# Batch 0's output in four accumulators, begun before batch 1's second attention, and output work shared out anew over the slots

## Chip, core and metric

One core of one Trainium2 chip runs the whole program. The metric is the time of one execution on the device in microseconds (us), lower is better. The kernel before takes 245.6 us, the median of three runs (245.07, 245.60 and 245.72).

## What is computed

Eight batches of 8 heads, 576 positions, head size 64. Each batch goes through two attentions: 32 learned queries `p` read keys and values and give 32 packed vectors per head, and then the real queries read these packed vectors as keys and as values. The rows of all batches (4608 x 512) go through a layer of 512 to 2048 to 512 with the function `h cos(h)` between.

```python
p_packed = sm_attn(p, k, v)              # sm_attn: softmax(scale * q @ k.T) @ v
out      = sm_attn(q, p_packed, p_packed)
x = out.transpose(0, 2, 1, 3).reshape(B * S, H * D)
h = x @ w_in
return (h * cos(h)) @ w_out
```

## The kernel before, in words

All matmuls are in bf16 with fp32 sums. The order of instructions is written out by hand: each engine runs its own in the order of the source, and only waits on data and buffers move them against each other.

**Per batch.** `s1` makes the scores of the first attention (TensorE, L143) and their exponentials (ScalarE, L152); `a1_pe` or `a1_xbar` transposes them, `pp` (L186) multiplies with v, `pp_T` (L198) transposes the packed vectors. `ppw` (L213) multiplies these with a quarter of `w_in` at once and writes `PPW`, so that the second attention's product and the first layer become one matmul. `s2` makes the scores of the second attention (L143), whose exponentials `a2u` (L231) are summed over keys by a matmul with ones (`sums2`, L239), then logarithm (L241), exponential (L247) and the product on VectorE (L249) give the normalised `a2n`.

**A slot.** `slot(s)` makes the hidden layer of batch s in 16 steps, one for each 128 of the 2048 hidden features. A step is four matmuls of 288 columns (`h_mm`, L263), the cosine on ScalarE (L267) and the product on VectorE (L270), which writes `gT`. Batch 0 is special: `h_one` makes 512 of its 576 positions (L289, L294, L295), in single banks, and `h_rest` the other 64 later (L303, L307, L309).

**The output and the filler.** `out_gen(b)` makes the output of a batch in chunks of 128 rows, each of 16 matmuls of 128x512 (L351), a copy to SBUF and a store. It is a generator: `fill(n)` takes its next n matmuls, wherever the source calls it. `slot` spreads its share evenly over its 16 steps (`quota`), more of it at steps that are `heavy`, and leaves `keep` matmuls over; `hooks` are other work put behind a step. An odd batch has a fifth chunk with the last 64 rows of two batches, which comes from `joint`. Batch 0's chunks 0 and 1 run interleaved by quarters of `w_out`, chunks 2 and 3 after them.

**Banks.** PSUM has eight banks here. Two (`O`) hold output chunks, and are borrowed through `bank`; the other six are either three pairs in turn (`psa`) or six single ones (`one`). `banks` switches between the two. A hidden product takes a pair.

**Loads.** They are issued by GpSimd (POOL) in the source's order (`load`, `load_w_in`, `load_w_out`). `xbar` transposes a batch's q or k by DMA from SyncE (SP), which also issues the stores, and `behind` lets POOL wait until such a transpose has landed. Batches 0 and 1 have their q, and batches 0 to 2 their k, transposed on TensorE instead (`pe_T`, L116); `pack_p` transposes the learned queries (L131).

**Around the change.** After batch 0's hidden layer come warm-up matmuls on zeros (`warm`, L391), the transposes of batch 1's q, a table load on ScalarE and `s2(1)`. The filler of batch 0 is set just ahead of `s2(1)`. Slot 1 has as hooks the second half of batch 1's `ppw`, `h_rest(0)`, `pack_p`, two transposes by DMA and the rest of batch 2's k. The lines that decide when the output begins:

```python
    warm(4, one())
    pe_T("q", 1, (ACT, V, V), (0,), own=one)
    ACT.preload_act_table_set(EXP_SET)
    pe_T("q", 1, (ACT, V, V), (1, 2), own=one)
    rest15()
    warm(3, one())
    ...
    banks(3)
    set_filler(0)
    s2(1)
    ppw(1, 0, V)
    fill(4)
```

Of the kernel before, what the change touches and what calls it, by code (L numbers as in the profile page):

```python
# [15 lines left out]
def kernel(  # L16
# [34 lines left out]
    ctx.enter_context(tc.manual_schedule())  # L51
    psum = {"stack": ctx.enter_context(ExitStack())}

    def banks(pairs):

        psum["stack"].close()
        if pairs:
            psum["A"] = psum["stack"].enter_context(tc.tile_pool(name="psA", bufs=pairs, space=PSUM))
        if pairs < 3:
            psum["H"] = psum["stack"].enter_context(tc.tile_pool(name="psH", bufs=6 - 2 * pairs, space=PSUM))  # L60

    banks(3)
# [20 lines left out]
    def copy(eng, out, in_):  # L83
        if eng is ACT:
            ACT.copy(out=out, in_=in_)  # L85
        else:
            eng.tensor_copy(out=out, in_=in_)  # L87

    def psa(dt=FP32):
        return psum["A"].tile([128, 2, 512 if dt == FP32 else 1024], dt, name="psA", tag="A")  # L90

    def load(n, b):
        bf[n, b] = bf_pool.tile([TP, H, C * D], BF16, name=n + "bf", tag=n + "bf", bufs=1 if n == "q" else 2)
        G.dma_start(out=bf[n, b], in_=srcs[n][b].rearrange("h (p c) d -> p h (c d)", c=C))
# [7 lines left out]
        nc.sync.dma_start_transpose(out=t, in_=bf[n, b].rearrange("p h x -> p (h x)"))  # L102

    def one(dt=FP32):
        return psum["H"].tile([128, 512 if dt == FP32 else 1024], dt, name="psH", tag="H")

    def pe_T(n, b, engs=(V, V, V), groups=(0, 1, 2), own=None):
        if 0 in groups:
# [14 lines left out]
    def bank(dt=FP32):  # L123
        return O.tile([128, 512 if dt == FP32 else 1024], dt, name="ot", tag="ot")
# [73 lines left out]
            nc.tensor.transpose(ps[:, i * 128:(i + 1) * 128], t[:, i * D:i * D + 128], ident)  # L198
        copy(eng, ppT[b % 2].rearrange("p i x n -> p (i x n)"), ps[:, 0:256])

    def ppw(b, n, eng=None, own=False, later=False, cuts=((0, 512),)):
        if b not in PPW:
            PPW[b] = ppw_pool.tile([128, 2, DF], BF16, name="PPW", tag="PPW")
        two = isinstance(eng, tuple)
        if own:
            ps = [bank(), bank()]
        else:
            t = psa()
            ps = [t[:, 0, :], t[:, 1, :]]
# [117 lines left out]

    def n_chunks(b):
        return 5 if b % 2 and b < B - 1 else 4

    def tail_chunk(b, c):
        osb = o_pool.tile([128, DM], FP32, name="osb")
        for i, (a, z) in enumerate(((0, 256), (256, 384), (384, 512))):
# [6 lines left out]
            for (a, z, rows), q in zip(pieces_of(b, c), (nc.sync, nc.scalar)):  # L340
                q.dma_start(out=rows[:, cols], in_=osb[a:z, cols])

    def out_gen(b):
        groups = [(0, 1), (2,), (3,)] if b == 0 else [(c,) for c in range(n_chunks(b))]
        for grp in groups:
            pss = {c: O.tile([128, DM], FP32, name="ot", tag="ot") for c in grp}
            for f0 in range(0, NFC, 4):
                for c in grp:
                    for fc in range(f0, f0 + 4):
                        w = joint[b // 2][:, fc, :] if c == 4 else gT[b][:, fc, c * 128:(c + 1) * 128]  # L350
                        nc.tensor.matmul(pss[c], w, w_out_bf[:, fc, :],  # L351
                                         start=(fc == 0), stop=(fc == NFC - 1))
                        if fc == NFC - 1:
                            osb = o_pool.tile([128, DM], FP32, name="osb")
                            copy(osb_eng[0], osb, pss[c])
                            for a, z, rows in pieces_of(b, c):
                                nc.sync.dma_start(out=rows, in_=osb[a:z, :])
                        yield

    filler = []  # L360

    def set_filler(b):
        filler.append([out_gen(b), 16 * n_chunks(b)])

    def to_do():
        return sum(n for _, n in filler)
# [58 lines left out]
    warm(1)  # L425
    pp_T(0)
    pe_T("q", 0, (V, ACT, V))
    load("q", 1)
    for n in range(4):
        load_w_out(n)  # L430
    G.dma_start(out=p_raw[:, 4:, :], in_=p_rows[:, 4:, :])
    load("k", 2)
# [7 lines left out]
    normalise(0)  # L440
    s1(1)
    ACT.preload_act_table_set(SIN_SET)
    cut_ppw, rest_ppw = ppw(0, 0, V, own=True, later=True, cuts=((0, 128), (128, 512)))
    warm(3, psa()[:, 0, :])
    cut_ppw()
    rest_ppw()
    banks(0)
    a1_pe(1, own=one)
    recips(1)
    for fc in range(13):  # L450
        h_one(0, fc)()()
        if fc in (0, 4, 8):
            ppw(0, 1 + fc // 4, (ACT, ACT if fc == 8 else V), own=True)
    c13 = h_one(0, 13)
    pp(1, ACT, own=bank)
    c13()()
    c14 = h_one(0, 14)
    c15 = h_one(0, 15, own=bank)
    pp_T(1, ACT, own=bank)
    c14()()  # L460
    rest15 = c15()
    warm(4, one())
    pe_T("q", 1, (ACT, V, V), (0,), own=one)
    ACT.preload_act_table_set(EXP_SET)
    pe_T("q", 1, (ACT, V, V), (1, 2), own=one)
    rest15()
    warm(3, one())
    load("k", 3)
    load("q", 2)
    load("v", 2)  # L470
    dup_p(4, 2 * B, G)
    banks(3)
    set_filler(0)
    s2(1)
    ppw(1, 0, V)
    fill(4)
    sums2(1, 0)
    fill(1)
    sums2(1, 1)
    rest_ppw, = ppw(1, 1, (V, V), later=True)  # L480
    fill(3)
    normalise(1)
    ACT.preload_act_table_set(SIN_SET)
    rest_ppw()
    fill(7)

    def slot(s, hooks, keep=0, heavy={}, last=None):


        left = to_do() - keep  # L490
        weight = [1 + heavy.get(fc, (0, 0))[0] for fc in range(NFC)]
        for fc in range(NFC):
            rest = h_mm(s, fc)
            if fc == NFC - 1 and last:
                last()
            rest()
            quota = (left * sum(weight[:fc + 1])) // sum(weight) - (left + keep - to_do())
            behind = min(quota, heavy[fc][1]) if fc in heavy else quota
            fill(quota - behind)
            while hooks and hooks[0][0] == fc:  # L500
                hooks.pop(0)[1]()
            fill(behind)
# [24 lines left out]
    def cross(n, b):  # L527
        return lambda: xbar(n, b)

    osb_eng[0] = ACT  # L530
    slot(1, [(2, lambda: pw2(1, 2, (ACT, V))), (4, lambda: h_rest(0)), (6, lambda: pack_p(2, 4)), (7, cross("k", 3)),
             (8, tk2), (9, cross("q", 2)), (10, lambda: pe_T("k", 2, (V, V, ACT), (2,)))], 4, {2: (1, 2), 4: (3, 5)})
    ACT.preload_act_table_set(EXP_SET)
    osb_eng[0] = V
    behind(xT["q", 2][0:1, 0, 0:1])
# [1 line left out]
    load("q", 3)  # L537
    load("k", 4)

    set_filler(1)  # L540
    fill(4)
    s1(2)
    fill(7)
# [28 lines left out]
        load(n, b)  # L572
    fill(9)
    osb_eng[0] = ACT
    slot(2, [(7, lambda: tiled(2))], 10, {7: (5, 4)}, lambda: pp_T(3, V))

    for s in range(3, B):
        nxt = s + 1 < B
        ACT.preload_act_table_set(EXP_SET)
        osb_eng[0] = V  # L580
        set_filler(s - 1)
# [64 lines left out]
```

## Time and profile before

| What | Value |
|---|---|
| Median of three runs | 245.6 us |
| The profiled execution | 245.1 us |
| Its span, first to last instruction | 243.3 us |
| Granted TensorE clock | 0.997 |
| TensorE busy | 233.8 us, 96% of the span |
| ScalarE, VectorE, GpSimd busy | 166.1, 162.0, 37.4 us |
| Output matmuls of 128x512 (L351) | 560, about 380 ns each as shown |
| Hidden products (L263) | 448 matmuls of 128x288 |
| Transfers | 37.37 MB in 64377 packets |

The span is what the trace covers; the execution is 1.8 us longer. A row of the timeline gives the start, the time from the first start to the last end, the engine, the source line, the operation, the tile written and the tiles read, the shape and how many there are; in brackets stands the idle time ahead of it and what ended it. Matmuls are pipelined: each is shown with its whole way through the array, so that 380 ns for one and 216 ns from one start to the next are no contradiction. The chain of waits is followed back from the last instruction, at each step to what released it.

### The profile page before, as it was taken

The numbers are of one execution on the slowest core, as the hardware profiler recorded it, in microseconds if no ns is written. First come the engines' busy times: TensorE is split into PE (matmuls) and PEld (weight loads), VectorE is DVE, ScalarE is ACT, GpSimd is POOL, SyncE is SP. The second block draws the span as 40 slices with busy tenths as digits, with TensorE's granted clock in tenths as the row PEclk, the third lists the DMA queues.
The fourth block names the chain that finished last, engine by engine and source line by source line (L and its number), as shares of the span: only waits on it lengthen the run. The fifth ranks groups of instructions, "written<-read, shape, count | busy, mean of one in ns | idle before, by whom it ended". The sixth has DMA issues, their size and how long they took to land.

```text
span 243.3 us, 5484 instructions
## 1 busy us (share of the span) xinstructions
PE 233.8 (96%) x2251; PEld 128.9 (53%) x2251; DVE 162.0 (67%) x256; ACT 166.1 (68%) x267; POOL 37.4 (15%) x60
## 2 busy tenths in 40 slices
PE   7789899999999999999999999999999999999994
PEld 3454354566446564556455654655455645665453
DVE  3259997787568795778758675868667878784001
ACT  2349999778478696868787687858796666773110
POOL 8432230210400041004100510030101010011000
PEclk9999999999999999999999999999999999999998
DMA  6999999999799999997999899999292111311133
GB/s 94 203 205 206 204 206 229 199 237 187 163 184 183 219 179 180 197 197 163 158 199 219 162 221 204 188 164 176 66 192 52 31 46 43 86 36 53 46 84 86
DMA packets 64377, 37.37 MB, mean 154 GB/s; under 512 B 36865, under 2 KB 59777, under 8 KB 64353
## 3 DMA queue, kind: packets, MB, share of 16 engines
q0 software_dynamic: 23152, 18.75, 51.0%
q1 hardware_dynamic: 40960, 18.16, 35.9%
q8 instruction: 17, 0.28, 0.4%
q10 hardware_dynamic: 240, 0.13, 0.2%
q14 instruction: 8, 0.06, 0.1%
HBM read 37.22 MB, written 9.44 MB: 192 GB/s over the span
## 4 chain that ended last, share of the span: by engine, by line
PE 82%; DVE 6%; ACT 1%; issue 1%; ACTq 0%
PE ot L351 50%; PE psA L263 22%; DVE gT L295 3%; PE psA L213 3%; PE psA L143 2%; PE psA L239 2%; PE ot L337 1%; PE psA L186 1%; DVE gT L270 1%; DVE PPW L87 1%; ACT cosT L267 1%; ACT cosT L294 0%; PE psA L116 0%; DVE qT L87 0%; PE psA L303 0%
## 5 line engine op out<-in xcount | busy, mean ns | idle before, releaser
L351 PE MATMUL ot<-w_out_bf,gT 128*128 128x512 bf16 x512 | 134.0, 379 | 0.0
L270 DVE TENSOR_TENSOR gT<-psA,cosT 128x576 bf16<-128x576 f32 x112 | 83.3, 757 | 21.0 <-ACT cosT L267 19.9
L267 ACT ACTIVATE cosT<-psA 128x576 bf16<-128x576 f32 x112 | 72.9, 652 | 24.9 <-PE psA L263 23.5
L263 PE MATMUL psA<-a2n,PPW 128*128 128x288 bf16 x448 | 73.3, 286 | 0.0
L351 PEld LDWEIGHTS <-gT 128*128 128x128 bf16 x512 | 48.2, 98 | 39.5 <-issue 4.2
L263 PEld LDWEIGHTS <-PPW 128*128 128x128 bf16 x448 | 43.8, 98 | 30.1 <-issue 0.4
L87 DVE CAST PPW<-psA 128x1024 bf16<-128x1024 f32 (+1 forms) x24 | 26.8, 1131 | 6.4 <-PE psA L213 6.2
L85 ACT COPY osb<-ot 128x512 f32<-128x512 f32 (+1 forms) x23 | 13.1, 569 | 16.2 <-PE ot L351 13.9
L87 DVE COPY osb<-ot 128x512 f32<-128x512 f32 (+2 forms) x15 | 9.7, 645 | 20.4 <-PE ot L337 17.2
L274 POOL COPY joint<-gT 128x512 bf16<-128x512 bf16 x14 | 8.6, 618 | 78.2 <-DVE gT L270 78.2
L249 DVE SCALAR_TENSOR_TENSOR a2n<-a2u,r,lns 128x576 bf16<-128x576 bf16 x16 | 12.4, 814 | 9.6 <-ACT lns L247 9.6
L152 ACT ACTIVATE a<-psA 128x576 bf16<-128x576 f32 x16 | 10.2, 646 | 8.2 <-PE psA L143 8.2
L241 ACT ACTIVATE lns<-psA 128x576 f32<-128x576 f32 x16 | 10.3, 650 | 7.2 <-PE psA L239 6.7
L351 PE MATMUL ot<-w_out_bf,joint 128*128 128x512 bf16 x48 | 12.2, 380 | 0.0
L98 POOL COPY gate<-kT 1x1 bf16<-1x1 bf16 x4 | 0.7, 180 | 72.7 <-DMA kT<-kbf 72.7
L231 ACT ACTIVATE a2u<-psA,rs 128x576 bf16<-128x576 f32 x16 | 11.0, 737 | 1.1 <-PE psA L143 1.0
L247 ACT ACTIVATE lns<-lns 128x576 f32<-128x576 f32 x16 | 10.0, 673 | 0.0
L213 PE MATMUL psA<-w_in_bf,ppT 64*32 64x512 bf16 x224 | 9.8, 379 | 0.0
L295 DVE TENSOR_TENSOR gT<-psH,cosT 128x512 bf16<-128x512 f32 x15 | 9.3, 680 | 0.4 <-ACT cosT L294 0.4
L391 PE MATMUL ot<-wz 128*128 128x512 f32 (+2 forms) x13 | 7.5, 661 | 1.9 <-DVE wz L404 1.7
L294 ACT ACTIVATE cosT<-psH 128x512 bf16<-128x512 f32 x15 | 8.4, 628 | 0.7 <-DVE gT L295 0.4
L289 PE MATMUL psH<-a2n,PPW 128*128 128x512 bf16 x30 | 7.8, 381 | 0.8 <-DVE PPW L87 0.8
(88 smaller groups left out, 170.6 us busy)
## 6 DMA issues: line engine op xcount, KB each, us to landing
kbf<-in_k_dram POOLq DMA_DIRECT2D x8, 576.0 KB, 14.0
vbf<-in_v_dram POOLq DMA_DIRECT2D x8, 576.0 KB, 7.8
qbf<-in_q_dram POOLq DMA_DIRECT2D x8, 576.0 KB, 10.9
out_dram<-osb SPq DMA_DIRECT2D x24, 192.0 KB, 2.6
out_dram<-osb SPq DMA_DIRECT2D x22, 128.0 KB, 2.9
w_in_bf<-in_moe_w_in_dram POOLq DMA_DIRECT2D x4, 512.0 KB, 17.3
w_out_bf<-in_moe_w_out_dram POOLq DMA_DIRECT2D x4, 512.0 KB, 20.8
out_dram<-osb SPq DMA_DIRECT2D x25, 64.0 KB, 2.3
```

The costliest lines, as they stand in the source:

```text
L85: ACT.copy(out=out, in_=in_)
L87: eng.tensor_copy(out=out, in_=in_)
L152: ACT.activation(out=a1[b % 2][:, y, :, 0:TP].rearrange("p (e m) x -> p e m x", e=2), in_=ps[y][:, :, 0:HS].rearrange("p e (m x) -> p e m ...
L213: nc.tensor.matmul(ps[y][32 * x:32 * x + 32, :], ppT[b % 2][r, 0, x, :], w_in_bf[r, x, n * 512:(n + 1) * 512], start=True, stop=True)
L231: ACT.activation(out=a2u[b][:, y].rearrange("p (e x) -> p e x", e=2), in_=ps[y][:, :, 0:HS], func=AF.Exp, scale=rs1[b][:, y:y + 1])
L241: ACT.activation(out=lns[b][:, y].rearrange("p (e x) -> p e x", e=2), in_=ps[:, :, 0:HS], func=AF.Ln)
L249: V.scalar_tensor_tensor(out=a2n[b][:, y], in0=a2u[b][:, y], scalar=r1[b][:, y:y + 1], in1=lns[b][:, y], op0=ALU.mult, op1=ALU.mult)
L263: nc.tensor.matmul(ps[:, e, 0:HS], PPW[b][:, y, fc * 128:(fc + 1) * 128], a2n[b][:, y, e * HS:(e + 1) * HS], start=(y == 0), stop=(y == 1))
L267: ACT.activation(out=csv, in_=ps[:, :, 0:HS], func=AF.Sin, bias=PI_HALF)
L270: V.tensor_tensor(out=gT[b][:, fc, :].rearrange("p (e x) -> p e x", e=2), in0=ps[:, :, 0:HS], in1=csv, op=ALU.mult)
L295: return lambda: V.tensor_tensor(out=gT[b][:, fc, 0:512], in0=ps, in1=cs, op=ALU.mult)
L351: nc.tensor.matmul(pss[c], w, w_out_bf[:, fc, :], start=(fc == 0), stop=(fc == NFC - 1))
```

## The change

Three things are changed.

- The first quarter of `w_out` is loaded ahead of batch 1's q instead of behind it.
- Batch 0's output is made by `out_first`, with all four chunks open at once. Chunks 0 and 1 take the two output banks, chunks 2 and 3 one of the three pairs, which is held (`at=2`) while the other work has two pairs in turn. The 64 matmuls go by quarters of `w_out`. They begin straight after batch 0's hidden layer; the seven warm-up matmuls there are gone, the first two `ppw` of batch 1 move ahead of its transposes and into single banks, and `c15` takes a single bank. 36 output matmuls stand ahead of slot 1 instead of 15. When chunk 3 is complete, ScalarE copies chunks 2 and 3 out and the third pair returns.
- Odd slots, and the last one, end with the first 7 or 8 matmuls of their own output: `slot` sets its own filler at step 10 (`trail`). Slot 1 gets a list of weights for its steps and its hooks stand later; what even slots leave over (`keep`) falls to 0 or 1.

The loads of later batches, the shapes and the arithmetic are the same. The diff, cut to its core:

```diff
+    pairs, turn = [], [0]
-    def banks(pairs):
+    def banks(kind):
         psum["stack"].close()
...
+        name, n = ("psA", 1) if kind == "pairs" else ("psH", 6)
+        psum[name] = psum["stack"].enter_context(tc.tile_pool(name=name, bufs=n, space=PSUM))
+        pairs[:], turn[0] = [0, 1, 2], 0
...
+    def psa(dt=FP32, at=None):
+        if at is None:
+            at = pairs[turn[0] % len(pairs)]
+            turn[0] += 1
+        return psum["psA"].tile([128, 2, 512 if dt == FP32 else 1024], dt, name="psA", tag=f"A{at}")
...
+    def out_first():
+        pss = {}
+        for c, fcs in ((0, 4), (1, 4), (2, 4), (3, 4), (0, 8), (1, 8), (2, 8), (3, 8),
+                       (2, 12), (3, 12), (2, 16), (3, 16), (0, 16), (1, 16)):
+            if c not in pss:
+                if c == 2:
+                    held = psa(at=2)
+                    pairs[:] = [0, 1]
+                pss[c] = O.tile([128, DM], FP32, name="ot", tag="ot") if c < 2 else held[:, c - 2, :]
+            for fc in range(8 if (c, fcs) in ((0, 16), (1, 16)) else fcs - 4, fcs):
+                nc.tensor.matmul(pss[c], gT[0][:, fc, c * 128:(c + 1) * 128], w_out_bf[:, fc, :],
+                                 start=(fc == 0), stop=(fc == NFC - 1))
+                if fc == NFC - 1 and c == 3:
+                    store(0, 2, pss[2])
+                    store(0, 3, pss[3])
+                    pairs[:], turn[0] = [0, 1, 2], 0
+                elif fc == NFC - 1 and c < 2:
+                    store(0, c, pss[c])
+                yield
...
+    load_w_out(0)
     load("q", 1)
-    for n in range(4):
+    for n in range(1, 4):
         load_w_out(n)
...
-    rest15 = c15()
-    warm(4, one())
-    pe_T("q", 1, (ACT, V, V), (0,), own=one)
+    c15()()
+    set_filler(0)
+    fill(4)
+    for n in range(2):
+        ppw(1, n, (ACT, V), own=one)
+    fill(4)
     ACT.preload_act_table_set(EXP_SET)
-    pe_T("q", 1, (ACT, V, V), (1, 2), own=one)
-    rest15()
-    warm(3, one())
+    banks("pairs")
+    fill(4)
+    t = psa(BF16)
+    for i in range(2):
+        pe_T("q", 1, (None,) * 3, (i,), own=lambda dt: t[:, i, :])
+    V.tensor_copy(out=xT["q", 1][:, 0:16].rearrange("p (i a) x -> p i (a x)", i=2), in_=t[:, :, 0:8 * TP])
+    pe_T("q", 1, (V, V, ACT), (2,))
...
+    fill(4)
     s2(1)
-    ppw(1, 0, V)
     fill(4)
     sums2(1, 0)
-    fill(1)
+    fill(2)
     sums2(1, 1)
-    rest_ppw, = ppw(1, 1, (V, V), later=True)
-    fill(3)
+    fill(10)
     normalise(1)
     ACT.preload_act_table_set(SIN_SET)
-    rest_ppw()
-    fill(7)
+    fill(4)
...
+            if fc == 10 and trail:
+                set_filler(s)
...
-    slot(1, [(2, lambda: pw2(1, 2, (ACT, V))), (4, lambda: h_rest(0)), (6, lambda: pack_p(2, 4)), (7, cross("k", 3)),
-             (8, tk2), (9, cross("q", 2)), (10, lambda: pe_T("k", 2, (V, V, ACT), (2,)))], 4, {2: (1, 2), 4: (3, 5)})
+    slot(1, [(5, lambda: pw2(1, 2, (ACT, V))), (6, lambda: h_rest(0)), (7, cross("k", 3)),
+             (8, lambda: pack_p(2, 4)), (9, cross("q", 2)), (10, tk2), (11, lambda: pe_T("k", 2, (V, V, ACT), (2,)))],
+         trail=8, heavy={5: (0, 2), 6: (0, 2)}, weight=[3, 3, 3, 3, 2, 3, 3, 2, 2, 2, 2, 2, 2, 2, 1, 1])
...
-    slot(2, [(7, lambda: tiled(2))], 10, {7: (5, 4)}, lambda: pp_T(3, V))
+    slot(2, [(7, lambda: tiled(2))], 0, {7: (5, 4)}, lambda: pp_T(3, V))
...
-            slot(s, [(7, lambda: tiled(s))], 5 if s % 2 else 13, {7: (5, 4)}, lambda: pp_T(s + 1, V))
+            slot(s, [(7, lambda: tiled(s))], 0 if s % 2 else 1, {7: (5, 4)}, lambda: pp_T(s + 1, V),
+                 7 if s % 2 else 0)
         else:
-            slot(s, [], 5)
-    set_filler(B - 1)
+            slot(s, [], trail=7)
     fill(1000)
```

More of the change, by code (lines that the diff above doesn't have):

```diff
@@ L52 @@
     psum = {"stack": ctx.enter_context(ExitStack())}
-    def banks(pairs):
+    pairs, turn = [], [0]
+    def banks(kind):
         psum["stack"].close()
[L57 to L62, printed above, removed]
+        name, n = ("psA", 1) if kind == "pairs" else ("psH", 6)
+        psum[name] = psum["stack"].enter_context(tc.tile_pool(name=name, bufs=n, space=PSUM))
+        pairs[:], turn[0] = [0, 1, 2], 0
+    banks("pairs")
     V, ACT, G = nc.vector, nc.scalar, nc.gpsimd
@@ L87, in copy @@
             eng.tensor_copy(out=out, in_=in_)
-    def psa(dt=FP32):
-        return psum["A"].tile([128, 2, 512 if dt == FP32 else 1024], dt, name="psA", tag="A")
+    def psa(dt=FP32, at=None):
[3 more added lines that the diff above has]
+        return psum["psA"].tile([128, 2, 512 if dt == FP32 else 1024], dt, name="psA", tag=f"A{at}")
     def load(n, b):
@@ L104, in one @@
     def one(dt=FP32):
-        return psum["H"].tile([128, 512 if dt == FP32 else 1024], dt, name="psH", tag="H")
+        return psum["psH"].tile([128, 512 if dt == FP32 else 1024], dt, name="psH", tag="H")
     def pe_T(n, b, engs=(V, V, V), groups=(0, 1, 2), own=None):
@@ L199, in pp_T, with ppw @@
         copy(eng, ppT[b % 2].rearrange("p i x n -> p (i x n)"), ps[:, 0:256])
-    def ppw(b, n, eng=None, own=False, later=False, cuts=((0, 512),)):
+    def ppw(b, n, eng=None, own=None, later=False, cuts=((0, 512),)):
         if b not in PPW:
@@ L205, in ppw @@
         if own:
-            ps = [bank(), bank()]
+            ps = [own(), own()]
         else:
@@ L341, in tail_chunk, with store @@
                 q.dma_start(out=rows[:, cols], in_=osb[a:z, cols])
-    def out_gen(b):
[L344 to L358, printed above, removed]
+    def store(b, c, ps):
+        osb = o_pool.tile([128, DM], FP32, name="osb")
+        copy(osb_eng[0], osb, ps)
+        for a, z, rows in pieces_of(b, c):
+            nc.sync.dma_start(out=rows, in_=osb[a:z, :])
@@ new lines, in out_gen @@
+    def out_gen(b):
+        for c in range(n_chunks(b)):
+            ps = O.tile([128, DM], FP32, name="ot", tag="ot")
+            for fc in range(NFC):
+                w = joint[b // 2][:, fc, :] if c == 4 else gT[b][:, fc, c * 128:(c + 1) * 128]
+                nc.tensor.matmul(ps, w, w_out_bf[:, fc, :], start=(fc == 0), stop=(fc == NFC - 1))
+                if fc == NFC - 1:
+                    store(b, c, ps)
+                yield
[17 more added lines that the diff above has]
+                    store(0, c, pss[c])
+                yield
@@ L360 @@
     filler = []
     def set_filler(b):
-        filler.append([out_gen(b), 16 * n_chunks(b)])
+        filler.append([out_gen(b) if b else out_first(), 16 * n_chunks(b)])
     def to_do():
@@ L442 @@
     ACT.preload_act_table_set(SIN_SET)
-    cut_ppw, rest_ppw = ppw(0, 0, V, own=True, later=True, cuts=((0, 128), (128, 512)))
+    cut_ppw, rest_ppw = ppw(0, 0, V, own=bank, later=True, cuts=((0, 128), (128, 512)))
     warm(3, psa()[:, 0, :])
@@ L446 @@
     rest_ppw()
-    banks(0)
+    banks("single")
     a1_pe(1, own=one)
@@ L452 @@
         if fc in (0, 4, 8):
-            ppw(0, 1 + fc // 4, (ACT, ACT if fc == 8 else V), own=True)
+            ppw(0, 1 + fc // 4, (ACT, ACT if fc == 8 else V), own=bank)
     c13 = h_one(0, 13)
@@ L457 @@
     c14 = h_one(0, 14)
-    c15 = h_one(0, 15, own=bank)
+    c15 = h_one(0, 15)
     pp_T(1, ACT, own=bank)
     c14()()
-    rest15 = c15()
-    warm(4, one())
-    pe_T("q", 1, (ACT, V, V), (0,), own=one)
-    ACT.preload_act_table_set(EXP_SET)
-    pe_T("q", 1, (ACT, V, V), (1, 2), own=one)
-    rest15()
-    warm(3, one())
+    c15()()
[4 more added lines that the diff above has]
+    fill(4)
+    ACT.preload_act_table_set(EXP_SET)
+    banks("pairs")
+    fill(4)
[4 more added lines that the diff above has]
+    pe_T("q", 1, (V, V, ACT), (2,))
     load("k", 3)
@@ L471, with slot @@
     dup_p(4, 2 * B, G)
-    banks(3)
-    set_filler(0)
+    fill(4)
     s2(1)
-    ppw(1, 0, V)
     fill(4)
     sums2(1, 0)
-    fill(1)
+    fill(2)
     sums2(1, 1)
-    rest_ppw, = ppw(1, 1, (V, V), later=True)
-    fill(3)
+    fill(10)
     normalise(1)
     ACT.preload_act_table_set(SIN_SET)
-    rest_ppw()
-    fill(7)
-    def slot(s, hooks, keep=0, heavy={}, last=None):
-        left = to_do() - keep
-        weight = [1 + heavy.get(fc, (0, 0))[0] for fc in range(NFC)]
+    fill(4)
+    def slot(s, hooks, keep=0, heavy={}, last=None, trail=0, weight=None):
+        left, done = to_do() - keep + trail, 0
+        weight = weight or [1 + heavy.get(fc, (0, 0))[0] for fc in range(NFC)]
         for fc in range(NFC):
@@ L496, in slot @@
             rest()
-            quota = (left * sum(weight[:fc + 1])) // sum(weight) - (left + keep - to_do())
+            if fc == 10 and trail:
+                set_filler(s)
+            quota = (left * sum(weight[:fc + 1])) // sum(weight) - done
+            done += quota
             behind = min(quota, heavy[fc][1]) if fc in heavy else quota
@@ L538 @@
     load("k", 4)
-    set_filler(1)
     fill(4)
@@ L580 @@
         osb_eng[0] = V
-        set_filler(s - 1)
+        if s % 2:
+            set_filler(s - 1)
         fill(5)
```

## The prediction, made before the result was known

> **What bounds the kernel now.** I read the page first, then the chain of waits in order of time, then the timeline of 30 to 52 us, where the change acts. A *fill* below is one 128x512 output matmul (L351); *fc* is one of a slot's 16 steps; the hidden product of a step is L263, its cosine L267, its product L270.
>
> ```profile
> PE 233.8 (96%) x2251; PEld 128.9 (53%) x2251; DVE 162.0 (67%) x256; ACT 166.1 (68%) x267; POOL 37.4 (15%) x60
> PE 82%; DVE 6%; ACT 1%; issue 1%; ACTq 0%
> ```
>
> TensorE is busy 96% and carries 82% of the chain that ended last. A busy share does not say how fast it streams, so I take the distance between starts:
>
> ```profile
> 42.44 0.49 PE psA L263 x4
> 46.95 0.93 PE psA L303 x32
> 220.68 15.54 PE ot L351 x72
> ```
>
> In the chain 72 fills take 15.54 us, 0.216 us each, and the four matmuls of a hidden product 0.49. From 40 us to the end TensorE goes from one to the next with waits of 0.25 us at most, so moving a fill from one full stretch to another is worth nothing. What can be won is time in which TensorE does nothing useful, and that lies before 40.2 us:
>
> ```profile
> 30.49 3.70 DVE L295 TENSOR_TENSOR gT<-psH,cosT 128x512 bf16<-128x512 f32 x6 [0.40 <-ACT cosT L294]
> 32.36 1.02 PE L391 MATMUL psH<-wz 128*128 128x512 bf16 x4
> 33.23 1.19 PE L116 MATMUL psH<-ident,qbf 96*128 96x96 bf16 x24
> 34.25 0.81 PE L391 MATMUL psH<-wz 128*128 128x512 bf16 x3
> 34.67 1.28 ACT L464 ACT_TABLE_LOAD   x1
> 35.86 1.04 PE L351 MATMUL ot<-w_out_bf,gT 128*128 128x512 bf16 x4
> ```
>
> Seven warm-up matmuls (L391) on zeros, 7 x 0.216 = 1.51 us, and the first fill only at 35.86. The 7.98 us from 32.25 to 40.23 hold 15 fills (3.24), 24 transposes (1.0), the scores (0.35), two PPW groups (0.67), the sums (0.49) and two small transposes (0.11): 5.86 useful, 2.12 lost. The slot's first hidden product then waits 0.20 more for a2n.
>
> **The change, part by part.** *Loads.* The trace's landings follow each other: batch 1's v at 8.47 + 21.6 = 30.1, q at 15.58 + 17.5 = 33.1, the quarters of w_out at 35.6, 38.1, 40.7, 43.3. One quarter takes 2.5, q 2.95. With the quarter in front it lands at 32.6 and q at 35.6; all later loads are unmoved. The quarter can be issued early: what holds the q load back on POOL until 15.58 is the buffer of batch 0's q, which the quarter does not need. Free, if q at 35.6 is early enough.
>
> *The stretch before slot 1*, laid out with the rows above: four fills from 32.7 to 33.56; two PPW groups of 0.335 (0.03 and a tail of 0.305) to 34.23; eight fills to 35.96. The transposes of q take over the banks of gT15 and of the second PPW cast, both on VectorE: gT14 ends at 34.19 as now (30.49 + 3.70), then 0.62 (3.70/6) and two casts of 0.64 (L87, 1.28 for two): 36.1. So q, landed at 35.6, has 0.5 of cover. Transposes to 37.14 (24 x 0.042), four fills to 38.0. The scores wait for the copies of q: ScalarE's 0.80 from 37.3 ends at 38.1; VectorE's one 128x1536 copy is not in the trace; between one 128x768 copy (0.56) and two (1.24), I take 0.97 from the slope of 0.29 for 256 and 0.56 for 768 columns, and ScalarE's hides it (at 1.24 it costs 0.1). Scores 38.15 to 38.5, four fills, sums from 39.45 (0.09 late, for a2u), two fills, sums, fourteen fills: slot 1 begins at 43.39. a2n: from a2u's start to the second half's end it took 35.97 to 40.64, 4.67; from 38.54 that gives 43.2, needed at 43.39 + 0.24. Cover 0.4; each tenth beyond costs a tenth.
>
> 36 fills are done where it was 15. 21 x 0.216 = 4.54, so the same point of the work was 40.43 + 4.54 = 44.97: **gain 1.58 us**.
>
> The Trainium skill (TensorE: Matmul & The Clock Gate, Back-to-back issue gap) gives a sustained 131 ns for a 512-column matmul; by that 21 fills were worth 2.75 and this stretch would lose 0.2, the total coming to 247.0. The trace has 216, 72 times in a row, and decides.
>
> *Slot 1, first four steps.* One pair of banks is held for chunks 2 and 3, so hidden products share two pairs. A pair is free again after 0.69 (41.36 to ScalarE's 42.05) + 0.65 + 0.03 + 0.76 + 0.06 = 2.19 us, 1.10 per step on two pairs; TensorE's step with three fills is 0.488 + 0.648 = 1.136. No wait, with 0.04 to spare.
>
> *Then the held pair is emptied by two ScalarE copies* (0.58 each, L85 row, back to back 1.11), which stand before the cosine of step 4. It starts at 49.3, not 48.7; its pair comes free at 50.8. The second of the two PPW groups (moved from step 2 to step 5) takes that pair and is reached at 50.1: **0.67 wait**, and 0.13 at step 5's own pair.
>
> *h_rest and pack_p.* They fall on the same pair again, in both kernels:
>
> ```profile
> 46.79 1.10 PE L303 MATMUL psA<-a2n,PPW 128*128 128x64 bf16 x32
> 47.92 1.02 ACT L307 ACTIVATE cosR<-psA 128x1024 bf16<-128x1024 f32 x1 [0.67 <-PE psA L303]
> 48.98 1.23 DVE L309 TENSOR_TENSOR joint<-psA,cosR 128x1024 bf16<-128x1024 f32 x1 [1.41 <-ACT cosR L307]
> 50.26 0.38 PE L131 MATMUL psA<-ident,p_bf 128*128 128x128 bf16 x4
> ```
>
> From h_rest's first matmul to the pair's release are 3.42 us (46.79 to 50.21). Before, TensorE had 0.93 + 5 fills + two products + 2 fills = 3.42 in between, just enough. After, it has 0.93 + 0.43 + 0.49 + 0.43 + 0.49 = 2.77: **0.7 wait** (0.05 now). That leaves VectorE behind, and I add 0.43 for three short waits on it later in the slot (0.06, 0.10, 0.27, laying out the rest of the slot the same way; laying out the old slot so gives its end within 0.02 of the trace's 60.95). Slot 1 thus waits 1.9 where it waited 0.1: **loss 1.8**.
>
> *The rest.* Fills between slots 1 and 2 are 44 as before, slot 2 has 28 for 30, slot 3 36 for 34, later slots the same; the tail 60 for 72, which are the 12 done earlier. In slot 2 an output copy no longer stands before step 6's cosine, so pp, which waited 0.2 for gT (82.15), waits 0.15 us: gain 0.1. The trails read gT of finished steps: step 15's product in the last slot is ready about 1.7 us after its matmuls, with ten fills, 2.2, in front of its use.
>
> Sum: -1.58 + 1.8 - 0.1 = +0.1. The profiled execution took 245.1 (span 243.3, 1.8 around it), so 245.2; the median of the three runs is 0.5 above it: **245.7 us**.
>
> **The rivals.** *Slot 1 does not wait* (faster). For: the old slot lost 0.1 us with more fills in it. Against: the pairs follow in a fixed turn, so both waits hang on distances read above. Without the two, 1.37 less: 244.35. Half of it is already beyond what can be measured.
>
> *Batch 1's softmax comes late* (slower). q now lands behind a quarter of w_out. It decides from q landing after 36.1, or the chain from the scores to a2n taking over 0.4 longer than now. ScalarE does everything in it, in order, behind two new PPW casts and the table load, from 33.3 to 43. q a microsecond late moves the scores by 0.5 and the slot with them after 0.4 is used, and the copies behind; with the chain 0.7 longer as well, 0.8 more: 246.5. Against: the loads in front of it land within 0.1 of an even beat.
>
> *Batch 3's a1 comes late* (slower). The transposes of k 3 and q 2 stand on SP behind chunk 0's store, so they begin at 55.9, not 51.1. k 3 took 6.68 to issue then, with two loads in flight, but 2.99 at 81.07. At 2.99 q 2 lands near 65 as now. At 6.68 all that is gated on it comes 4.6 later, the transposed a1 of batch 3 at 85.6 instead of 81.0, needed at 82.15 + 2.8 = 84.9: 0.7, 246.4. It decides from about 6 us.
>
> *The quarter does not land earlier*: then the first fill waits until 35.6 with nothing to put in its place, 2.9 us. The evenly spaced landings in order of issue speak against it.
>
> **How the numbers follow.** A run can tell 0.3%, 0.74 us, from no change. Forecast and its near surroundings (245.0 to 246.3) 0.46; no waits in slot 1, 0.26; late softmax 0.15; late a1 0.10; no earlier quarter 0.03. So faster 0.26, same 0.46, slower 0.28. The range takes in both near rivals and the unknown copy and covers: 244.0 to 247.0; below it lies a stretch before slot 1 that gains its whole 2.3 lost while slot 1 loses nothing.
>
> **What would show it.** No L391 rows after 30 us and the first fill at 32.7; 36 fills and the first L263 at about 43.4; in slot 1, waits of TensorE at the second PPW group and at pack_p of 0.6 to 0.7 each; 60 fills in the last stretch instead of 72. Wrong: q landing after 36.1, a2n after TensorE has run out of fills, or slot 1 without these waits.

## The result and the profile after

The changed kernel takes 245.92 us, the median of 17 runs (245.69 to 246.06). The kernel before, run beside it 17 times, takes 245.23 (245.02 to 245.72). The ratio is 1.0025 with a 95% interval of 1.0018 to 1.0033: slower by 0.7 us, inside what was called no change, and a little on the slow side of it. The profiled execution took 245.88 us with a span of 244.1, against 245.1 and 243.3 before: 0.78 more.

The page of the changed kernel, its busy line and its chain:

```profile
PE 230.0 (94%) x2208; PEld 128.1 (52%) x2244; DVE 161.3 (66%) x256; ACT 167.1 (68%) x267; POOL 37.6 (15%) x60
...
PE 79%; DVE 7%; ACT 2%; issue 2%; ACTq 0%
```

TensorE's seven warm-ups are gone, but its share of the chain fell from 82% to 79%, and VectorE and ScalarE have come in. (36 matmul records are missing from this trace, which lowers its busy sum.) So TensorE now waits for the other two somewhere. Line numbers have moved: the output matmul, a *fill*, is L375 for batch 0 and L359 for the others, the hidden product L268, PPW's matmuls L218, the casts and copies L86 on ScalarE and L88 on VectorE, the product to `gT` L300 for batch 0 and L275 for the others, `pack_p` L136. The timeline of the stretch before slot 1:

```profile
32.52 1.04 PE L375 MATMUL ot<-w_out_bf,gT 128*128 128x512 bf16 x4
...
33.48 0.63 PE L218 MATMUL psH<-w_in_bf,ppT 64*32 64x512 bf16 x16
...
34.04 1.04 PE L375 MATMUL ot<-w_out_bf,gT 128*128 128x512 bf16 x4
34.65 1.28 DVE L88 CAST PPW<-psH 128x512 bf16<-128x512 f32 x2
35.05 1.28 ACT L493 ACT_TABLE_LOAD   x1
35.99 1.04 PE L375 MATMUL psA<-w_out_bf,gT 128*128 128x512 bf16 x4 [0.91 <-DVE PPW L88]
36.86 1.19 PE L121 MATMUL psA<-ident,qbf 96*128 96x96 bf16 x24
...
42.58 1.55 DVE L254 SCALAR_TENSOR_TENSOR a2n<-a2u,r,lns 128x576 bf16<-128x576 bf16 x2 [3.83 <-ACT lns L252]
43.14 1.28 ACT L513 ACT_TABLE_LOAD   x1
44.15 0.65 PE L268 MATMUL psA<-a2n,PPW 128*128 128x288 bf16 x4
```

The first fill starts at 32.52, not 35.86: the quarter of `w_out` landed at 32.47. But eight fills and two PPW groups later, with the last start near 34.7, TensorE stands until 35.99, until VectorE's second PPW cast is done. At 0.216 us to a fill the eight are through at 34.90, so the wait is 1.09 (the row's 0.91 counts from the end of the last fill's way through the array). The chain, in order of time, runs through the same place:

```profile
30.43 4.30 DVE gT L300 x7
34.73 1.21 DVE PPW L88 x2
35.94 0.05 issue
35.99 1.04 PE psA L375 x4
37.02 1.02 PE psA L121 x24
```

The fill that waits writes chunk 2, into the held pair, and the cast that it waits for reads another bank, going by the order in which the source hands the banks out; the trace has no bank numbers. In slot 1 the two places of the prediction wait:

```profile
48.90 1.08 ACT L86 COPY osb<-psA 128x512 f32<-128x512 f32 x2
...
49.74 0.65 PE L268 MATMUL psA<-a2n,PPW 128*128 128x288 bf16 x4
...
50.54 0.41 PE L218 MATMUL psA<-w_in_bf,ppT 64*32 64x512 bf16 x8
...
51.37 0.41 PE L218 MATMUL psA<-w_in_bf,ppT 64*32 64x512 bf16 x8 [0.42 <-DVE gT L275]
...
55.05 1.22 DVE L314 TENSOR_TENSOR joint<-psA,cosR 128x1024 bf16<-128x1024 f32 x1 [0.77 <-ACT cosR L312]
...
56.33 0.38 PE L136 MATMUL psA<-ident,p_bf 128*128 128x128 bf16 x4 [0.53 <-DVE joint L314]
```

The held pair is emptied by two copies from 48.90, the second PPW group waits, and `pack_p` waits for `h_rest`'s product to leave its pair. Slot 1, from its first hidden matmul to its last, took 19.82 us, with 36 fills; before it took 19.95 with 45.

### The profile page after: what moved, and what is told of

The parts are those of the page before. It is cut to its first block, busy times and chain, and to the rows that moved or that the text cites. A ratio compares the mean times of both kernels' runs of the same rounds, so it can differ in the third digit from the quotient of the medians.

```text
span 244.1 us, 5438 instructions
## 1 busy us (share of the span) xinstructions
PE 230.0 (94%) x2208; PEld 128.1 (52%) x2244; DVE 161.3 (66%) x256; ACT 167.1 (68%) x267; POOL 37.6 (15%) x60
## 3 DMA queue, kind: packets, MB, share of 16 engines
q1 hardware_dynamic: 40960, 18.16, 34.7%
## 4 chain that ended last, share of the span: by engine, by line
PE 79%; DVE 7%; ACT 2%; issue 2%; ACTq 0%
PE ot L359 43%; PE psA L268 22%; DVE gT L300 3%; PE psA L375 3%; PE psA L218 2%; PE psA L148 2%; PE ot L375 1%; PE ot L342 1%; PE psA L244 1%; DVE PPW L88 1%; DVE gT L275 1%; PE psA L191 1%; ACT cosT L272 1%; PE psA L121 1%; DVE joint L314 1%
## 5 line engine op out<-in xcount | busy, mean ns | idle before, releaser
L359 PE MATMUL ot<-w_out_bf,gT 128*128 128x512 bf16 x424 | 109.8, 379 | 2.1 <-issue 1.6
L275 DVE TENSOR_TENSOR gT<-psA,cosT 128x576 bf16<-128x576 f32 x112 | 83.2, 757 | 21.9 <-ACT cosT L272 20.9
L268 PE MATMUL psA<-a2n,PPW 128*128 128x288 bf16 x448 | 73.2, 286 | 0.4
L359 PEld LDWEIGHTS <-gT 128*128 128x128 bf16 x448 | 42.2, 98 | 37.4 <-issue 4.2
L268 PEld LDWEIGHTS <-PPW 128*128 128x128 bf16 x448 | 43.7, 98 | 30.2 <-issue 0.9
L88 DVE CAST PPW<-psA 128x1024 bf16<-128x1024 f32 (+1 forms) x21 | 24.3, 1170 | 7.9 <-PE psA L218 7.9
L88 DVE COPY osb<-ot 128x512 f32<-128x512 f32 (+2 forms) x17 | 11.0, 647 | 15.6 <-PE ot L342 14.6
L86 ACT COPY osb<-ot 128x512 f32<-128x512 f32 (+1 forms) x19 | 10.8, 568 | 14.3 <-PE ot L359 9.1
L359 PE MATMUL ot<-w_out_bf,joint 128*128 128x512 bf16 x45 | 14.0, 379 | 0.3 <-issue 0.2
L300 DVE TENSOR_TENSOR gT<-psH,cosT 128x512 bf16<-128x512 f32 x16 | 9.9, 685 | 0.4 <-ACT cosT L299 0.4
L218 PE MATMUL psA<-w_in_bf,ppT 64*32 64x512 bf16 x208 | 9.2, 380 | 0.4 <-DVE gT L275 0.4
L299 ACT ACTIVATE cosT<-psH 128x512 bf16<-128x512 f32 x16 | 8.9, 633 | 0.7 <-DVE gT L300 0.4
L375 PE MATMUL ot<-w_out_bf,gT 128*128 128x512 bf16 x30 | 8.8, 380 | 0.1
```

Source lines behind the costliest of these rows:

```text
L268: nc.tensor.matmul(ps[:, e, 0:HS], PPW[b][:, y, fc * 128:(fc + 1) * 128], a2n[b][:, y, e * HS:(e + 1) * HS], start=(y == 0), stop=(y == 1))
L275: V.tensor_tensor(out=gT[b][:, fc, :].rearrange("p (e x) -> p e x", e=2), in0=ps[:, :, 0:HS], in1=csv, op=ALU.mult)
L300: return lambda: V.tensor_tensor(out=gT[b][:, fc, 0:512], in0=ps, in1=cs, op=ALU.mult)
L359: nc.tensor.matmul(ps, w, w_out_bf[:, fc, :], start=(fc == 0), stop=(fc == NFC - 1))
L375: nc.tensor.matmul(pss[c], gT[0][:, fc, c * 128:(c + 1) * 128], w_out_bf[:, fc, :], start=(fc == 0), stop=(fc == NFC - 1))
```

## The experiments

Theory after this trace: the change wins less ahead of slot 1 than forecast, because the switch from six single banks to three pairs waits for every user of the single ones; and it pays in slot 1 because TensorE, with fewer fills there, only reaches the pairs before ScalarE and VectorE let them go. Rivals: the wait at 35.99 is for the held pair's own banks; and the loss in slot 1 is a matter of where fills are counted. "Before" is the run of the kernel before beside each experiment.

**1. The switch earlier.** The eight fills of chunks 0 and 1 stand together, the switch comes ahead of the PPW groups, and these write pairs.

```diff
-    fill(4)
+    fill(8)
+    banks("pairs")
     for n in range(2):
-        ppw(1, n, (ACT, V), own=one)
-    fill(4)
+        ppw(1, n, (ACT, V))
     ACT.preload_act_table_set(EXP_SET)
-    banks("pairs")
```

> The changed kernel, but the six single banks are handed back to pairs before the two PPW groups of batch 1 and not behind them, so that what the pairs wait for on VectorE is the last product of batch 0 (gT15, ends at 34.75 in the changed kernel's trace) and no longer the second PPW cast behind it (ends at 35.93). Theory (the handover costs what the prediction missed: the first fill of chunk 2 at 35.99 though the one before it was through at 34.90): the transposes of q begin at 36.4 instead of 36.86, slot 1 at 43.7 instead of 44.15, and the time falls by 0.45 us, to about 245.4. Rival (q, which lands at 35.41 behind the quarter of w_out, holds the transposes and the softmax behind them): nothing moves, 245.9.

Measured: 245.86 us, ratio 1.0027 (1.0011 to 1.0044). The wait at the switch is 0.3 long, but the next step is late. Timeline:

```profile
32.31 2.50 DVE L300 TENSOR_TENSOR gT<-psH,cosT 128x512 bf16<-128x512 f32 x4
...
32.82 1.90 PE L375 MATMUL ot<-w_out_bf,gT 128*128 128x512 bf16 x8 [0.32 <-DMA w_out_bf<-in_moe_w_out_dram]
...
34.86 0.62 PE L218 MATMUL psA<-w_in_bf,ppT 64*32 64x512 bf16 x16
35.34 1.07 ACT L86 CAST PPW<-psA 128x512 bf16<-128x512 f32 x2 [1.36 <-PE psA L218]
...
35.95 1.29 DVE L88 CAST PPW<-psA 128x512 bf16<-128x512 f32 x2 [1.15 <-ACT PPW L86]
...
36.70 1.18 PE L121 MATMUL psA<-ident,qbf 96*128 96x96 bf16 x24 [0.24 <-DVE PPW L88]
```

The eight fills are through at 34.55, and PPW's first group starts at 34.86, behind VectorE's last product of batch 0, which ends at 34.80. That group writes the first pair. If the six single banks are handed out in turn, as the source asks for them, its two banks last held the hidden products of steps 10 and 11, which are done before the four shown, of steps 12 to 15, begin at 32.31. So it waits for a user of other banks.

VectorE's cast reads the other bank of the pair, yet starts only when ScalarE's cast of the first is done: in the compiled program it waits for that cast, while with single banks it waits for the matmul alone (in run 3 the two start at 38.69 and 38.72, each released by its matmul). Slot 1 starts at 43.93 instead of 44.15, and the total does not show it beyond its spread. That the switch waits for all its users is borne out; the cure traded it for another wait.

**2. Only the load order, in the kernel before.**

```diff
+    load_w_out(0)
     load("q", 1)
-    for n in range(4):
+    for n in range(1, 4):
         load_w_out(n)
```

> The kernel before with only the load order changed (first quarter of w_out ahead of batch 1's q). Theory: q lands at 35.4 instead of 33.05, nothing is there to fill the time, and the transposes, the scores and the softmax of batch 1 begin 2.3 us later: 245.2 + 2.2 = 247.4, with TensorE's wait on q in front of the transposes. Rival (the second attention of batch 1 is set by ScalarE and not by q): within 0.5 us of before.

Measured: 247.95 us, ratio 1.0109 (1.0085 to 1.0134). TensorE waited 2.13 us for q; and then something not in the expectation. Timeline, then stretches with the granted clock in the column behind the engines:

```profile
35.39 1.19 PE L116 MATMUL psH<-ident,qbf 96*128 96x96 bf16 x24 [2.13 <-DMA qbf<-in_q_dram]
...
38.73 1.73 PE L351 MATMUL ot<-w_out_bf,gT 128*128 128x512 bf16 x4
```

```profile
32.00:36.00 4.00, 1.87 (x21) 1.10 (x21) 2.07 (x4) 1.89 (x6) 0.00 (x0) 1.00 1.28 206
36.00:40.00 4.00, 3.89 (x45) 1.44 (x43) 2.70 (x4) 3.40 (x4) 1.53 (x2) 0.59 1.24 206
```

From 36.76 the clock is granted at half for 3.41 us; four fills take 1.73 instead of 1.04. Slot 1 starts 3.4 later than before (43.61 against 40.23), more than the wait alone. This execution took 248.55 at a mean granted clock of 0.993, and one other of the six, 249.39, has the same clock. The other four were granted 1.000 and took 247.34 to 248.01, which is 2.0 to 2.7 above the 245.36 of the kernel before beside them and close to the expected 247.4.

**3. Only the load order undone, in the changed kernel.** The three lines above the other way.

> The changed kernel with the old load order. Theory: the first quarter lands at 35.5, the first fill waits until then instead of 32.5, all behind it on TensorE waits too; the wait for the banks (1.1 us) falls into that time, so 3.0 - 1.1 = 1.9 us slower than the changed kernel, 247.8. Rival (the early fills only fill waits that are there anyway): below 0.5 us.

Measured: 249.61 us, ratio 1.0174 (1.0135 to 1.0212). Stretches:

```profile
32.00:36.00 4.00, 0.53 (x4) 0.19 (x2) 2.83 (x5) 2.00 (x6) 0.03 (x1) 0.78 1.25 207
36.00:40.00 4.00, 3.82 (x23) 1.02 (x24) 1.28 (x2) 1.29 (x3) 0.00 (x0) 0.50 1.24 208
40.00:44.00 4.00, 4.00 (x51) 2.15 (x48) 0.97 (x2) 1.86 (x2) 0.77 (x2) 0.86 1.22 238
```

TensorE is empty for 3.65 us, and the clock is at half for 6.83 us, from 34.27. This execution took 251.08. The six are of two kinds: three were granted a mean clock of 0.986 to 0.990 and took 250.57 to 251.14, three were granted 0.997 or 0.998 and took 248.43 to 248.65; the median lies between and is no execution's time. So without the half clock the late quarter costs 2.5 to 2.7 us against the 245.92 of the changed kernel, more than the expected 1.9 and near the 2.9 that the prediction gave it; with the half clock it costs 4.7 to 5.2. The early quarter is what the new order stands on.

**4. No slot ends with its own output.**

```diff
-         trail=8, heavy={5: (0, 2), 6: (0, 2)}, ...
+         heavy={5: (0, 2), 6: (0, 2)}, ...
...
-        if s % 2:
-            set_filler(s - 1)
+        set_filler(s - 1)
```

Slot 1 keeps 28 fills, slot 2 leaves 10 over, and the later ones leave 5 or 13.

> The changed kernel without its trails: every slot makes output of earlier batches only, as before; slot 1 then has 28 fills and the last stretch 69. Theory by bookkeeping (a fill is worth 0.216 us wherever TensorE streams): 8 fills go from slot 1 to the end and the time stays, 245.9. Rival (the trail keeps TensorE from falling behind ScalarE and VectorE in slot 1, which with 28 fills has 16.7 us of matmuls for 16 us of ScalarE's work): 0.5 to 1.0 us slower.

Measured: 249.29 us, ratio 1.0153 (1.0135 to 1.0172). Eight fills fewer, 1.73 us of work, and slot 1 took 20.33 us instead of 19.82. Two of its waits:

```profile
51.81 0.41 PE L218 MATMUL psA<-w_in_bf,ppT 64*32 64x512 bf16 x8 [0.73 <-DVE gT L275]
...
57.11 0.38 PE L136 MATMUL psA<-ident,p_bf 128*128 128x128 bf16 x4 [0.53 <-DVE joint L314]
```

What the expectation called the theory, that the trail is bookkeeping, fell; its rival held, and by more than it gave. Fills taken out of slot 1 do not shorten it: its length, about 20 us, is set by the order in which ScalarE and VectorE empty the pairs, as what releases its waits shows, and fills only fill the gaps. The time of the missing fills turns up at the end: of the 3.21 us by which this span is longer, 2.59 are twelve more fills behind the last slot, and 0.62 is what the last slot ends later.

**5. Chunk 2 emptied when it is complete**, ahead of chunk 3's last quarter, so that only one copy stands at step 4.

```diff
-                if fc == NFC - 1 and c == 3:
+                if fc == NFC - 1 and c == 2:
                     store(0, 2, pss[2])
+                elif fc == NFC - 1 and c == 3:
                     store(0, 3, pss[3])
```

> The changed kernel, but chunk 2 is copied out when it is complete, in step 2 of slot 1, and not together with chunk 3 in step 3. Theory (the two ScalarE copies in a row delay step 4's cosine and with it the pair that the second PPW group of step 5 waits for, 0.5 us in the changed kernel): laid out with the same rows that wait falls to 0.1 but 0.27 comes back at step 6's own pair, so 0.25 us faster, 245.65. Rival (the copies are not what delays it): the wait stays at 0.5.

Measured: 246.72 us, ratio 1.0045 (1.0027 to 1.0063): slower, where faster was expected. Timeline:

```profile
47.03 0.59 PE L375 MATMUL psA<-w_out_bf,gT 128*128 128x512 bf16 x2
...
47.78 0.58 ACT L86 COPY osb<-psA 128x512 f32<-128x512 f32 x1
...
48.41 0.38 PE L375 MATMUL psA<-w_out_bf,gT 128*128 128x512 bf16 x1 [0.78 <-ACT osb L86]
```

The next fill, into chunk 3's bank, waits for the copy of chunk 2's bank. It is the behaviour of run 1 again, with TensorE and ScalarE: the two banks of one pair are one tile, and the program orders any use of it. The Trainium skill (PSUM — Partial Sum Buffer, PSUM bank collisions raise a hardware error) asks for a guard by bank and quadrant, not by address; these runs have a guard by tile, which is wider, and its price here is 0.95 us: at 0.216 to a fill the two are through at 47.46, and the next starts at 48.41.

**6. `pack_p` one step later**, at step 9.

> The changed kernel with pack_p one step later (behind step 9, not 8). Theory (from step 5 to 12 slot 1 is held by the chain of ScalarE, VectorE and three pairs, so a wait taken away in one place stands in the next): the 0.7 at pack_p turns into waits of 0.2 to 0.3 at step 9, at pack_p and at the next transposes, and the time stays at 245.9. Rival (the wait at pack_p is one isolated hole): 0.4 faster, 245.5.

Measured: 246.08 us, ratio 1.003 (1.0011 to 1.0049). As expected, the wait at `pack_p` is gone and TensorE waits elsewhere: 0.26 us ahead of step 9's hidden product and 0.37 at k's transposes. Slot 1 took 19.91. A wait that comes from TensorE being ahead moves when its place is moved.

**7. `h_rest` last**, on top of run 5: `pack_p` at step 6, k's transposes at 8 and 10, `h_rest` at 12.

> The changed kernel with chunk 2 copied out at once, h_rest moved to step 12 behind the other hooks (pack_p at 6, the transposes of k at 8 and 10) and the same 36 fills shifted towards steps 12 to 14. Theory (what slot 1 loses comes from h_rest's long ScalarE and VectorE work, followed by a user of its pair 2.8 us later): waits in slot 1 fall from 1.7 to 0.9 and the time by 0.8 to 1.0 us, to about 245.0. Rival (slot 1 is as long as ScalarE's and VectorE's work in it, in whatever order): no change, 245.9.

Measured: 246.09 us, ratio 1.0026 (1.0009 to 1.0043). Against run 5, its base, that is 0.63 faster: `pack_p` waits for nothing. But the 0.95 of run 5 is in it, slot 1 took 20.11, and the expected 245.0 was missed by 1.1.

**8. Runs 7 and 1 together.**

> The last one and the earlier handover of the banks together. Theory (the two losses, 1.1 us at the handover and 1.7 us in slot 1, are independent of each other): 1.3 to 1.5 us faster than the changed kernel, 244.5, and so 0.8 us faster than the kernel before. Rival (the handover's gain was lost again in e1 for a reason inside the program): as the last one, 245.0.

Measured: 245.96 us, ratio 1.0015 (0.9995 to 1.0035). 0.13 below run 7, which lies within the spread of either: slot 1 starts at 44.03 and again takes 20.11. Neither the expected 244.5 nor the rival's 245.0 came, since run 7, on which both rest, had already missed.

**9. More fills in slot 1.** If the waits are gaps, work put into them is free.

```diff
-            if fc == 10 and trail:
+            if fc == 8 and trail:
...
-         trail=8, heavy={5: (0, 2), 6: (0, 2)}, weight=[3, 3, 3, 3, 2, 3, 3, 2, 2, 2, 2, 2, 2, 2, 1, 1])
+         trail=13, heavy={5: (0, 2), 6: (0, 2), 8: (0, 1)},
+         weight=[3, 3, 3, 3, 2, 5, 3, 3, 4, 2, 2, 2, 2, 2, 1, 1])
```

Slot 2 and the later even ones get `trail` 5, the later odd ones 12 instead of 7, so that each does as many fills as it did.

> Slot 1 of the changed kernel takes five more output matmuls (41 instead of 36): two more at step 5, ahead of and behind the PPW groups, and three more at step 8, ahead of pack_p; its own output begins in it from step 8 with 13 matmuls instead of 8. All later slots do as many as they did, each ending five further into its own output, so that the stretch after the last slot has five fewer. Theory (TensorE waits in slot 1 because it is sent ahead of the pairs that ScalarE and VectorE still hold, so work put there is free): the waits of 0.49 at the second PPW group and 0.69 at pack_p fall to 0.2 and 0 to 0.1, the slot is as long as before to within 0.3 us or shorter by up to 0.3 (laid out by hand it ends 0.27 earlier), and the total falls by five fills, 1.08 us, and that: 244.6 to 244.9, and so 0.2 to 0.3% faster than the kernel before. Rival (ScalarE and VectorE set the slot's length in another way, or the output copies that come with the fills push the cosines further): the slot is longer by the five fills, 1.08 us, and the total stays at 245.9. Second rival: the deeper starts into a slot's own output wait for its products in later slots, 0.2 us in each of seven slots: 246 or more.

Measured: 247.44 us, ratio 1.009 (1.0076 to 1.0104). Slot 1 did exactly what the theory said: with five fills more it took 19.64 us, 0.18 less than with 36, and neither PPW nor `pack_p` waits noticeably. The total was lost behind the odd slots, where the second rival had its place:

```profile
63.84 0.59 PE L359 MATMUL ot<-w_out_bf,gT 128*128 128x512 bf16 x2
64.84 0.39 PE L359 MATMUL ot<-w_out_bf,gT 128*128 128x512 bf16 x1 [0.40 <-DVE gT L275]
65.54 0.61 PE L359 MATMUL ot<-w_out_bf,gT 128*128 128x512 bf16 x2 [0.32 <-DVE gT L275]
```

With 13 fills of a chunk done, the next ones are fc 13 to 15, and the products of the slot's last steps are not there. The stage from slot 1 to slot 2 took 14.76 us instead of 13.69, those behind slots 3 and 5 10.61 instead of 10.09.

**10. The second PPW group cast by ScalarE alone**, ahead of the switch.

```diff
-        ppw(1, n, (ACT, V), own=one)
+        ppw(1, n, (ACT, (V, ACT)[n]), own=one)
```

> The changed kernel with one edit: the second of the two PPW groups ahead of slot 1 is cast by ScalarE in both halves, instead of one half on each engine. Theory (the switch from six single banks to three pairs waits until every user of the single ones is done, and the last was VectorE's second cast at 35.93): ScalarE's third cast ends at 35.4 to 35.6, the first fill of chunk 2 starts at 35.5 to 35.6 instead of 35.99, slot 1 at 43.7 to 43.8 instead of 44.15, and the total falls by 0.3 to 0.4 to 245.5 to 245.6. Rival (only the held pair's own two banks count, and what was waited for there is another thing): the first fill of chunk 2 stays at 35.9 to 36.0 and the total at 245.9. Second rival: ScalarE, which also loads its table and copies q's transposes next, is later by the extra cast, 0.55, and hands all of it to the scores: slot 1 at 44.2 or later.

Measured: 245.71 us, ratio 1.0023 (1.0014 to 1.0032). Timeline:

```profile
34.21 1.56 ACT L86 CAST PPW<-psH 128x512 bf16<-128x512 f32 x3 [0.30 <-PE psH L218]
34.30 1.04 PE L375 MATMUL ot<-w_out_bf,gT 128*128 128x512 bf16 x4
34.66 0.68 DVE L88 CAST PPW<-psH 128x512 bf16<-128x512 f32 x1
...
35.82 1.02 PE L375 MATMUL psA<-w_out_bf,gT 128*128 128x512 bf16 x4 [0.49 <-ACT PPW L86]
```

VectorE's last cast is done by 35.35, and the fill now waits for ScalarE's third cast, 35.77: the switch follows whichever user is last, as the theory says, and on either engine. The wait from the end of the eight fills fell from 1.09 to 0.66. Of that 0.26 was lost because the quarter landed at 32.72 in this run, not 32.47; slot 1 starts 0.18 earlier, and the total stands 0.59 above the kernel before where the changed kernel stood 0.69 above. That 0.1 lies within the spread of the runs (245.38 to 245.97), so that the expected fall of 0.3 to 0.4 in the total is not shown.

**11. Runs 9 and 10 together.**

> Both edits of the two runs beside it: the five more output matmuls in slot 1 and the second PPW group cast on ScalarE alone. Theory: the two stages do not touch each other, so the gains add up: 1.0 to 1.3 and 0.3 to 0.4 below the changed kernel, 244.2 to 244.6, faster than the kernel before by 0.3 to 0.5%. Rival (the later start of the softmax's chain takes back the second gain): as the run with the five matmuls alone, 244.6 to 244.9. If neither cure works, 245.9.

Measured: 247.29 us, ratio 1.0085 (1.0071 to 1.0099): run 9's loss, with 0.15 off, which is again within the spread. The expected 244.2 to 244.6 did not come. Slot 1 ran from 43.80 to 63.43.

**12. Run 11, with two chunks at once** at the start of an odd batch's output.

```diff
+        parts, pss = [(c, 0, NFC) for c in range(n_chunks(b))], {}
+        if b % 2:
+            parts[:2] = [(0, 0, 8), (1, 0, 8), (0, 8, NFC), (1, 8, NFC)]
```

> The run with both cures, and the output of each odd batch begins with two chunks at once (fc 0 to 7 of chunk 0, fc 0 to 7 of chunk 1, then the rest of both), so that the 12 or 13 output matmuls that end an odd slot use fc up to 7 alone and the next ones fc 4 to 7, instead of running straight on into fc 12 to 15. Theory (the five matmuls were free in slot 1, which ended 0.35 to 0.5 earlier with five more in it, and what made those two runs slower were waits behind the odd slots: TensorE waited there for the products of the slot's last steps, 1.07 us behind slot 1 and 0.5 behind each of slots 3, 5 and 7): these waits go, the stage between slots 1 and 2 takes 13.7 again instead of 14.8 and those behind slots 3 and 5 10.1 instead of 10.6; slot 2 starts near 77.2, the stretch after the last slot has five matmuls fewer, and the total is 244.2 to 244.6, below the kernel before by 0.2 to 0.4%. Rival (the longer stage behind slot 1 is something else than these waits, such as the softmax chain on ScalarE): it stays at 14.5 or more and the total at 245 to 247.

Measured: 244.86 us, ratio 0.9986 (0.9969 to 1.0003). It is 0.27 below the kernel before, where the changed kernel was 0.69 above; the interval just takes in no change. What followed slot 1 now runs on:

```profile
63.53 1.24 PE L364 MATMUL ot<-w_out_bf,gT 128*128 128x512 bf16 x5
64.70 0.44 PE L148 MATMUL psA<-kT,P 64*32 64x288 bf16 x16
65.07 1.68 PE L364 MATMUL ot<-w_out_bf,gT 128*128 128x512 bf16 x7
...
75.35 0.69 DVE L88 COPY osb<-ot 128x512 f32<-128x512 f32 x1
75.96 1.54 DVE L254 SCALAR_TENSOR_TENSOR a2n<-a2u,r,lns 128x576 bf16<-128x576 bf16 x2
...
77.09 0.86 PE L268 MATMUL psA<-a2n,PPW 128*128 128x288 bf16 x4
```

The stage takes 13.69 again, and 55 fills are left behind the last slot. The expected 244.2 to 244.6 was missed by 0.3: slot 2 took 14.93 instead of 14.66, 0.2 of it in the line at 77.09 (0.86 for 0.66). There VectorE copies a chunk out, 0.69 from 75.35, just ahead of a2n, which starts at 75.96. In runs 4 and 9 the copy stands there too, and the line takes 0.81 and 0.86; in the changed kernel and the one before it stands behind a2n (at 77.77 in the changed one), and the line takes 0.66 and 0.65. So the place of the copy goes with the 0.2 in all five, though no run moved the copy alone.

## Why the prediction was nearly right, and where it was not

The forecast was +0.1 in the profiled execution and 245.7; measured are +0.78 and 245.92. Two errors of opposite sense made the second number look better than the first. The 0.5 that was added for the median of three runs was chance: over 17 runs the kernel before has a median of 245.23. That the forecast missed by 0.22 and not by the 0.68 of the profiled execution is therefore luck.

**The stretch before slot 1** is the step that failed: gain 0.82 instead of 1.58. Slot 1 starts at 44.15, not 43.39. The quarter (32.47, forecast 32.6), q (35.41, forecast 35.6), the copy of 1536 columns (0.96, taken as 0.97) and the start of the fills were right. Wrong was "eight fills to 35.96", which lets chunk 2 begin without a wait. The prediction made q's transposes wait for VectorE's second cast until 36.1, and put eight fills ahead of them, four of which use the held pair. It gave these four no wait for their banks at all. But the switch waits for all users of the old banks, so they wait too, 1.09 us, and only then come the transposes, at 36.86. Run 10 shows this by moving the last user to another engine; run 1 by moving the switch. What no trace shows directly is which bank is which.

**Slot 1**: loss 1.58 (waits of 1.7, less the 0.12 of before) instead of 1.8; the mechanism was right at each place. Step 5's pair 0.13 (0.13), second PPW group 0.49 (0.67), `pack_p` 0.69 (0.7), the rest 0.4 (0.43), the first four steps none, 1.14 from one to the next. Runs 4 and 9 show what the waits are:

| Kernel | Fills in slot 1 | Its length, us |
|---|---|---|
| Before (no pair held) | 45 | 19.95 |
| Run 9 | 41 | 19.64 |
| Changed | 36 | 19.82 |
| Run 4 | 28 | 20.33 |

The kernel before has its other work at other steps and no pair held, so the three rows below it are the comparison. From 28 to 41 fills, 2.8 us of work, the length falls by 0.7 instead of growing. The nine fills that the change took out of slot 1 cost TensorE 1.94 us ahead of it, and slot 1 is 0.13 shorter without them.

**The rest** lost 0.03 where 0.1 of gain was expected in slot 2: there pp waits 0.18, not 0.15, and the later slots are as before. So -0.82 + 1.58 + 0.03 = +0.79. One side figure of the prediction leaves a term out: its 247.0 at 131 ns a fill is without the 0.5 for the median, with which it is 247.5.

**The rivals.** Slot 1 without waits fell. The late softmax fell: a2n's second half ends at 44.13 and is needed 0.24 behind 44.15, so 0.26 of the 0.4 of cover is left. The late a1 of batch 3 fell: the transposes of k 3 began at 56.44 (forecast 55.9) but took 3.49 to issue, below the 6 from which it would decide. That the quarter lands no earlier fell (32.47), and run 3 prices it at 2.5 to 2.7 at full clock, near the 2.9 that was given.

What stays open: whether `h_rest` last, without run 5's wait, is worth its 0.63 in the changed kernel; and a version with chunks 2 and 3 in separate tiles, which would free both of run 5's and run 1's orders, was not tried.

## What to carry to other kernels

Moving work out of a stage gains only if that stage was waiting for the work: read the stage's length with more and with less of it before counting the moved time as won. When a pool of banks is closed and another opened, count every user of the old one, on every engine, and not the banks that the next instruction writes; and count two banks of one tile as one. Work done ahead from a slot's own results needs a look at what stands behind the slot, where it runs straight into the results that come last.

## What was not expected of the hardware

- A TensorE wait of 2.13 us, behind warm-ups and ahead of 24 transposes, was followed by 3.41 us of half clock in the trace of run 2, and one of 3.65 us by 6.83 us, two times 3.41, in that of run 3. By the mean granted clock only two of run 2's six executions and three of run 3's six show such a loss; what decides which, no run here shows. The Trainium skill (TensorE: Matmul & The Clock Gate, HAM oscillation) asks for no idle gap above about 3.4 us; here 2.13 was followed by half clock in two of six. In the changed kernel, whose longest wait in this stretch is 0.91 as the trace counts it, the clock stayed at full, and all 17 executions were granted 0.997 or more. Single executions of run 1 (247.67), run 6 (248.10) and the kernel before (247.12) were granted 0.984 to 0.986 as well; of these there is no trace.
- The same load landed at times 0.8 us apart: the first quarter of `w_out` at 32.44 (run 9) to 33.21 (run 6), in kernels whose code up to there is the same. Before, TensorE had warm-ups there; now the first fill waits for it, 0.33 in run 10 and 0.73 in run 6.
